# Laying the score masks of the second half of the heads with ScalarE instead of VectorE

## The chip, the core and the metric

The kernel runs on one core of a Trainium2 chip. The metric is the device time of one execution in microseconds (us), lower is better. One execution of the kernel before was also taken with the hardware profiler; all readings of single instructions come from it. PE is TensorE, PEld its weight loads, DVE is VectorE, ACT is ScalarE, POOL is GpSimd, SP is SyncE, which issues most DMAs.

## What is computed

Two layers of the same kind, one after the other: a recurrent attention with a small memory, and a dense block, each with a residual. Between segments the attention is sequential: the memory that segment s leaves is part of the input of segment s+1.

```python
def A(x, mem0, Wq, Wk, Wv, Wo):          # S=2048, Dm=512, H=32 heads of Dh=128, M=8, seg=32
    mask = (idx[:, None] < M) | (idx[:, None] >= idx[None, :])     # 40 x 40
    mem = mem0
    for s in range(64):
        h = concat([mem, x[32*s : 32*s+32]])                       # 40 rows
        q, k, v = h @ Wq, h @ Wk, h @ Wv                           # per head
        scores = where(mask, q @ k.T * Dh**-0.5, -1e9)
        o = (softmax(scores) @ v) @ Wo
        mem = o[:M];  outs.append(o[M:])
x = x + A(layernorm(x));  x = x + relu(layernorm(x) @ w1) @ w2     # w1: 512 x 1376
x = x + A(layernorm(x));  x = x + relu(layernorm(x) @ w1) @ w2     # the same weights again
```

## The kernel before

**Steps.** The kernel makes 68 steps k = 0 to 67. In step k the first layer works on segment k and the second layer on segment k-4 (DELTA, line 18), so that both recurrences run side by side. Steps 0 to 3 have the first layer alone, 64 to 67 the second alone; the 60 steps 4 to 63 have both, and are called two-layer steps here. A matrix product then serves both layers at once: its moving operand has 80 columns (two times 40) instead of 40.

**Halves and batches.** The 32 heads are taken in two halves of 16 (`hf` = 0 and 1). For each half `qk` (line 546) makes the queries and keys in three batches of 6, 6 and 4 heads (line 544). A batch n (`qk_batch`, line 524) is a group of Wq products into one PSUM bank, copied to SBUF as QT by ACT (line 538), and a group of Wk products into another bank, copied as KT by DVE (line 540). The banks come from the pool `ps_c`, which has three (line 60); six groups of a half go through these three banks, so each group from the fourth on must wait until an earlier one has been copied out. In the second half of a step the instructions as built, with their waits, give this pairing: the Wk products of the second batch wait for ACT's copy of the first batch, the Wq products of the third batch wait for ACT's copy of the second batch, and the Wk products of the third batch wait for DVE's copy of the first batch. The changed kernel has the same three waits.

**Masks and scores.** Each layer has one score bank (`sp_tiles`, made in lines 208 to 213), 128 partitions by 320 columns of float32, held for the whole kernel. Before the scores are made, a mask (0 or -30000) is copied into the bank from the bf16 tile `maskb2` (`masks`, line 556), and the score products (`scores`, line 560, products in line 566) are then added onto it. `softmax` (line 577) reads the bank twice on DVE: the row maximum (line 582) and the subtraction of it into the SBUF tile `es` (line 586). ACT takes the exponential (line 588), DVE the row sums (line 593), reciprocals (line 594), and POOL or DVE the product with them (line 598). After the subtraction the score bank is free for the next mask.

**Where the masks stand.** The masks of the first half are laid at the end of the step before, in `normalize_step` (line 270, and line 804 for step 0). Those of the second half are laid inside `qk(1, ...)`, lines 552 and 553: the first layer's after batch 1 of the three, the second layer's after batch 2.

**Order.** PE, DVE, SP and POOL keep the order in which the program is written (lines 950 and 951). ACT is not among these: the framework orders ACT's instructions itself, with those made under `high_priority` (`PRIO`, line 19) ahead of others. In step k the first half is made by `qk(0)`, `scores`, `softmax` (lines 856 to 870); then `qk(1)` (line 880), some dense or output products (lines 881 to 887), and `scores` and `softmax` of the second half (lines 889 and 890). So the exponentials of the first half and the copies of the second half's queries stand close together in ACT's queue.

Of the kernel before, what the change touches and what calls it, by code (L numbers as in the profile page):

```python
# [22 lines left out]
def kernel(  # L23
# [14 lines left out]
    nc = tc.nc  # L38
# [138 lines left out]
    maskb2 = maskb[:].unsqueeze(1).to_broadcast([128, 8, L])  # L177
# [30 lines left out]
    sp_banks, sp_tiles = [], []  # L208
# [59 lines left out]
    def normalize_step(k):  # L268
        mom = stat_tail(stats_all) if norm_parts(k) else None
        masks(*layers(k))  # L270
        def rows():
            for eng, R, lo, hi in norm_parts(k):
                normalize(eng, XN, R, mom, lo, hi)


        if len(layers(k)) == 1:
            norm_rows[k] = rows
        else:
            rows()
# [244 lines left out]
    def qk_batch(n, h0, nh, a_lo, a_hi, between=None):  # L524
        ncol = (a_hi - a_lo) * L
        res = []
        for W_sb, nm in ((Wq_sb, "QT"), (Wk_sb, "KT")):
            qp = ps_c.tile([128, HB, 2 * L], F32, tag="c")
            for hi in range(nh):
                h = h0 + hi  # L530
                for c4 in range(NC4):
                    nc.tensor.matmul(qp[:, hi, 0:ncol], lhsT=W_sb[:, c4, h * Dh:(h + 1) * Dh],  # L532
                                     rhs=HT[:, c4, a_lo:a_hi, :], start=(c4 == 0), stop=(c4 == NC4 - 1))
            dst = wk.tile([128, nh, 2 * L], BF, tag=f"{nm}{n}", bufs=1, name=nm)
            if nm == "QT":
                if between:
                    between()
                nc.scalar.copy(out=dst[:, 0:nh, a_lo * L:a_hi * L], in_=qp[:, 0:nh, 0:ncol])  # L538
            else:
                nc.vector.tensor_copy(out=dst[:, 0:nh, a_lo * L:a_hi * L], in_=qp[:, 0:nh, 0:ncol])  # L540
            res.append(dst)
        return res
# [3 lines left out]
    def qk(hf, act, between=None, behind=None):  # L546
        res = []
        for n, (o, nh) in enumerate(BATCHES):
            res.append((o, nh) + tuple(qk_batch(n, 16 * hf + o, nh, act[0], act[-1] + 1, None if n else between)))
            if n == 0 and behind:  # L550
                behind()
            if hf and n > 0:
                masks(*act[n - 1:n])
        return res

    def masks(*act):
        for a in act:
            nc.vector.tensor_copy(out=sp_tiles[a], in_=maskb2)  # L558

    def scores(qks, act):  # L560
        for a in act:
# [237 lines left out]
    def first_step():  # L799


        slots = iter([w1_flat[:, 512 * i:512 * i + 512] for i in range(NC4 * Dff // 512)] +
                     [w2_flat[:, 512 * i:512 * i + 512] for i in range(8)])
        masks(0)
        with tc.high_priority(offset=PRIO):
            qks = qk(0, [0])
            scores(qks, [0])
            softmax(0, [0], True)
# [9 lines left out]
            values0(3, 2, stage=next(slots))  # L818
            load_x(1)
            qks = qk(1, [0], between=lambda: values0(5, 0, stage=next(slots)))  # L820
            scores(qks, [0])
            softmax(1, [0], True)
# [18 lines left out]
    def step(k):  # L841
# [9 lines left out]
        with tc.high_priority(offset=PRIO):  # L851
            behind = norm_rows.pop(k, None)
            if k == 1:
                def behind():
                    normalize(nc.vector, xbs[n_x], xbs[n_x], moments_x(n_x), 0, 128)
            qks = qk(0, act, behind=behind)
            load_values(k, act)
            if k == 1:
                memory_values(k)
                inputs_T(n_x, True)  # L860
# [169 lines left out]
```

## Time and profile before

| | us |
|---|---|
| median of 3 runs | 1603.49 |
| the runs | 1601.55 to 1604.02 |
| the profiled execution, its own time | 1601.33 |
| its span, first to last instruction | 1599.6 |
| PE busy in it | 1568.4 |
| DVE busy | 1262.8 |
| ACT busy | 737.9 |
| POOL busy | 346.7 |

The mean granted clock of TensorE was 0.998 of full speed. In the listings, a row of the timeline gives start, length, engine, line, operation, output and inputs, the count of instructions merged into it, and in brackets the idle time before it with what ended that. The length of an instruction reaches into the start of the next one on its engine where two run back to back, so the difference of two starts is what one costs an engine that has more to do.

### The profile page before, as it was taken

The page shows a single profiled execution, that of the slowest core. Times are in us where ns is not written, and L with a number is a line of the kernel's source. Part 1 is how long each engine was busy: PE and PEld are TensorE (multiplying, and loading weights), DVE is VectorE, ACT ScalarE, POOL GpSimd, SP SyncE. Part 2 cuts the span into 40 slices and gives each one's busy share as a digit, 9 for nine tenths or more (in the row PEclk, how much of TensorE's full clock was granted, in tenths as well). Part 3 has the DMA queues.
Part 4 walks back from the last instruction along what each step waited for, and adds up shares of the span by engine and source line. Part 5 has one row for each costly group of instructions (what it writes and reads, how often), then busy time and mean ns, then how long its engine had stood idle before and what let it go on. Part 6 is the DMA issues. An engine that isn't in the chain of part 4 may idle for free.

```text
span 1599.6 us, 94752 instructions
## 1 busy us (share of the span) xinstructions
PE 1568.4 (98%) x42718; PEld 1323.1 (83%) x42718; DVE 1262.8 (79%) x3112; ACT 737.9 (46%) x1800; POOL 346.7 (22%) x666
## 2 busy tenths in 40 slices
PE   5999999999999999999999999999999999999998
PEld 3677888888888888888888888888888898888876
DVE  4578888888888888888888888878888888787865
ACT  3434444444544444454444445445444544545442
POOL 2012222222222222222222222222222222222210
PEclk9999999999999999999999999999999999999999
DMA  9733343343344434434333433343343333334231
GB/s 367 238 78 77 72 94 85 68 91 86 88 66 91 88 65 93 86 80 75 91 86 64 96 86 81 77 90 89 64 101 81 79 77 80 87 67 100 70 68 38
DMA packets 222532, 146.38 MB, mean 92 GB/s; under 512 B 123976, under 2 KB 216496, under 8 KB 222128
## 3 DMA queue, kind: packets, MB, share of 16 engines
q1 hardware_dynamic: 218976, 136.09, 37.7%
q8 instruction: 335, 5.49, 1.5%
q0 software_dynamic: 3072, 4.20, 1.2%
q14 instruction: 69, 0.57, 0.1%
q10 hardware_dynamic: 80, 0.03, 0.0%
HBM read 65.41 MB, written 45.35 MB: 69 GB/s over the span
## 4 chain that ended last, share of the span: by engine, by line
PE 95%; DMA 2%; DVE 1%; SPq 1%; issue 1%; ACT 1%; POOLq 0%; ACTq 0%; DVEq 0%
PE qp L532 37%; PE wox L365 10%; PE wo L574 8%; PE vm L717 7%; PE v L346 7%; PE hp L468 6%; PE sp L491 5%; PE pv L634 4%; PE sp L566 4%; PE vp L306 3%; DMA Wv_sb<-in_A_Wv_dram 2%; PE tp L608 1%; PE xp L439 1%; PE wox L388 1%; SPq L134 0%
## 5 line engine op out<-in xcount | busy, mean ns | idle before, releaser
L538 ACT CAST QT<-qp 128x480 bf16<-128x480 f32 (+3 forms) x408 | 201.1, 493 | 392.9 <-PE qp L532 390.6
L532 PE MATMUL qp<-HT,Wk_sb 128*128 128x80 bf16 (+1 forms) x8704 | 369.3, 199 | 2.3 <-DVE KT L540 1.3
L532 PE MATMUL qp<-HT,Wq_sb 128*128 128x80 bf16 (+1 forms) x8704 | 369.6, 200 | 1.5 <-POOL HT L706 1.2
L532 PEld LDWEIGHTS <-Wq_sb 128*128 128x128 bf16 x8704 | 326.1, 99 | 32.9 <-issue 25.6
L532 PEld LDWEIGHTS <-Wk_sb 128*128 128x128 bf16 x8704 | 328.5, 100 | 3.8 <-issue 2.7
L540 DVE CAST KT<-qp 128x480 bf16<-128x480 f32 (+3 forms) x408 | 225.0, 565 | 100.8 <-PE qp L532 98.6
L598 POOL TENSOR_TENSOR P_sb<-es,sm 128x320 bf16<-128x320 f32 x185 | 130.6, 719 | 753.0 <-ACT es L588 510.4
L365 PE MATMUL wox<-Wo_sb,OTx 128*64 128x256 bf16 x2880 | 173.6, 273 | 0.0
L582 DVE TENSOR_REDUCE mx<-sp 128x8 f32<-128x320 f32 x256 | 114.8, 487 | 72.6 <-PE sp L566 71.7
L593 DVE TENSOR_REDUCE sm<-es 128x8 f32<-128x320 f32 x256 | 118.9, 464 | 45.4 <-ACT es L588 35.4
L365 PEld LDWEIGHTS <-OTx 128*64 128x64 bf16 x2880 | 150.2, 110 | 2.9
L588 ACT ACTIVATE es<-es 128x320 f32<-128x320 f32 x256 | 110.5, 468 | 57.9 <-DVE es L586 57.2
L717 PE MATMUL vm<-Wv_sb,HTm 128*32 128x512 bf16 x2176 | 136.2, 380 | 0.6 <-DVE HT L786 0.6
L346 PE MATMUL v<-Wv_sb,xnT 128*32 128x512 bf16 x2048 | 129.2, 378 | 0.2 <-issue 0.2
L574 PE MATMUL wo<-Wo_sb,OTm 128*32 128x512 bf16 x2144 | 128.7, 380 | 0.0
L558 DVE CAST sp<-maskb 128x320 f32<-128x320 bf16 x256 | 118.3, 484 | 0.0
L586 DVE TENSOR_TENSOR es<-sp,mx 128x320 f32<-128x320 f32 x256 | 113.7, 483 | 1.5
L717 PEld LDWEIGHTS <-HTm 128*32 128x32 bf16 x2176 | 90.3, 96 | 27.7 <-issue 12.6
L491 PE MATMUL sp<-w_sb,hT 128*64 128x256 bf16 (+4 forms) x1474 | 105.6, 276 | 0.6 <-ACT hT L474 0.5
L468 PE MATMUL hp<-xnT,w_sb 128*128 128x64 bf16 (+3 forms) x2948 | 103.4, 194 | 0.6 <-ACT xnT L986 0.3
L721 ACT CAST VmS<-vm 128x512 bf16<-128x512 f32 x134 | 78.4, 585 | 53.8 <-PE vm L717 53.8
L468 PEld LDWEIGHTS <-w_sb 128*128 128x128 bf16 (+1 forms) x2948 | 96.3, 101 | 1.8 <-issue 1.2
(113 smaller groups left out, 2025.4 us busy)
## 6 DMA issues: line engine op xcount, KB each, us to landing
Vs<-vd SPq DMA_DIRECT2D x96, 256.0 KB
vd<-vst SPq DMA_DIRECT2D x181, 128.0 KB
vmd<-VmS SPq DMA_DIRECT2D x134, 128.0 KB
Vs<-vmd SPq DMA_DIRECT2D x254, 32.0 KB
Vs<-vmd SPq DMA_DIRECT2D x60, 128.0 KB
Wq_sb<-in_A_Wq_dram SPq DMA_DIRECT2D x2, 2048.0 KB
Wk_sb<-in_A_Wk_dram SPq DMA_DIRECT2D x2, 2048.0 KB
Wv_sb<-in_A_Wv_dram SPq DMA_DIRECT2D x2, 2048.0 KB
```

The lines of the kernel that those rows point to most:

```text
L346: nc.tensor.matmul(vp[32 * j:32 * j + 32, :], lhsT=tokens[:, c4, :], rhs=Wv_sb[:, c4, n * 512:(n + 1) * 512], start=(c4 == 0), stop=(c4 == ...
L365: nc.tensor.matmul(out[64 * j:64 * j + nr, 0:256], lhsT=lhsT, rhs=rhs[:, 256 * j:256 * j + 256], start=start, stop=stop, tile_position=(0, ...
L468: nc.tensor.matmul(hp[0:fs, fc - f0, 0:n], lhsT=w1_sb[:, c4, fc * 128:fc * 128 + fs], rhs=cols(c4), start=(c4 == 0), stop=(c4 == NC4 - 1))
L491: nc.tensor.matmul(sp_banks[bank][64 * j:64 * j + n, 0:w], lhsT=hT_tiles[d][0:fs, fc, 0:n], rhs=w2_flat[0:fs, fc * Dm + 256 * j:fc * Dm + ...
L532: nc.tensor.matmul(qp[:, hi, 0:ncol], lhsT=W_sb[:, c4, h * Dh:(h + 1) * Dh], rhs=HT[:, c4, a_lo:a_hi, :], start=(c4 == 0), stop=(c4 == NC4 ...
L538: nc.scalar.copy(out=dst[:, 0:nh, a_lo * L:a_hi * L], in_=qp[:, 0:nh, 0:ncol])
L540: nc.vector.tensor_copy(out=dst[:, 0:nh, a_lo * L:a_hi * L], in_=qp[:, 0:nh, 0:ncol])
L558: nc.vector.tensor_copy(out=sp_tiles[a], in_=maskb2)
L574: nc.tensor.matmul(wo[32 * j:32 * j + 32, :], lhsT=OTm[:, h, n, 2 * M * c:2 * M * c + 4 * M], rhs=Wo_sb[:, h, :], start=(h < 4), stop=(h > ...
L593: nc.vector.tensor_reduce(out=sm[:], in_=es[:], axis=AX.X, op=ALU.add)
L598: eng.tensor_tensor(out=P, in0=es[:], in1=sm[:].unsqueeze(2).to_broadcast([128, 8, L]), op=ALU.mult)
L717: nc.tensor.matmul(vp[32 * j:32 * j + 32, :], lhsT=HTm[:, c4, :], rhs=Wv_sb[:, c4, n * 512:(n + 1) * 512], start=(c4 == 0), stop=(c4 == NC ...
```

## The change

The second half's masks get ScalarE's copy in place of VectorE's. The first layer's mask (the first of `act`) is laid after batch 0 instead of batch 1, the second layer's after batch 1 instead of batch 2. The masks of the first half stay as they are.

```diff
             res.append((o, nh) + tuple(qk_batch(n, 16 * hf + o, nh, act[0], act[-1] + 1, None if n else between)))
             if n == 0 and behind:
                 behind()
-            if hf and n > 0:
-                masks(*act[n - 1:n])
+            if hf:
+                masks(*act[n:n + 1], copy=nc.scalar.copy)
         return res
 
-    def masks(*act):
+    def masks(*act, copy=nc.vector.tensor_copy):
         for a in act:
-            nc.vector.tensor_copy(out=sp_tiles[a], in_=maskb2)
+            copy(out=sp_tiles[a], in_=maskb2)
```

In the program as built, 128 copies leave DVE's queue and 128 come into ACT's. Nothing else changes its place on any engine. In each of the 60 two-layer steps ACT's queue then reads: QT copy of batch 0, two exponentials, the two masks, QT copy of batch 1, QT copy of batch 2. In the one-layer steps it has one exponential and one mask, in steps 1, 2, 3 and 64 to 67 ahead of the QT copy of batch 1.

## Prediction

> **What bounds the kernel now.** I read the page first, then windows of 100 us for the share of each engine, then the waits of PE, and last the timelines of PE and ACT in one two-layer step.
>
> ```profile
> span 1599.6 us, 94752 instructions
> PE 1568.4 (98%) x42718; PEld 1323.1 (83%) x42718; DVE 1262.8 (79%) x3112; ACT 737.9 (46%) x1800; POOL 346.7 (22%) x666
> ...
> PE 95%; DMA 2%; DVE 1%; SPq 1%; issue 1%; ACT 1%; POOLq 0%; ACTq 0%; DVEq 0%
> ```
>
> PE is busy for 98% of the span, and 95% of the chain that ended last is PE. The windows say where the other 2% lies: of 400 to 500 us PE is busy 99.99 us, of 1000 to 1100 us 99.97, of 1300 to 1400 us 100.00. The idle 31 us are mostly in the start, before the weights are there. So in the 60 two-layer steps time is won only where a product takes less time or waits less, and every wait that is put before PE is paid in full. DVE, from which the change takes work, bounds nothing there:
>
> ```profile
> DVE KT L540 <- PE qp L532: 98.6, 135, 5.3
> DVE mx L582 <- PE sp L566: 71.7, 136, 1.5
> ```
>
> It waits 99 us for PE's queries and keys, and 72 us for the scores. In the other direction all waits of PE after the start are small: for DVE's KT 1.5 us in 6 times, for DVE's part of the probabilities 2.1 us in 3.
>
> Now the place of the change. In the step that starts at 787 us the second half's queries and keys run from 792.91 us (ACT first, then PE, then DVE; start, length, engine, line):
>
> ```profile
> 794.03 0.56 ACT L538 CAST QT<-qp 128x480 bf16<-128x480 f32 x1 [2.12 <-PE qp L532]
> 794.49 0.83 ACT L588 ACTIVATE es<-es 128x320 f32<-128x320 f32 x2
> 795.75 0.56 ACT L538 CAST QT<-qp 128x480 bf16<-128x480 f32 x1 [0.43 <-PE qp L532]
> 797.19 0.42 ACT L538 CAST QT<-qp 128x320 bf16<-128x320 f32 x1 [0.88 <-PE qp L532]
> ```
>
> ```profile
> 792.91 1.03 PE L532 MATMUL qp<-HT,Wq_sb 128*128 128x80 bf16 x24
> 793.78 1.03 PE L532 MATMUL qp<-HT,Wk_sb 128*128 128x80 bf16 x24
> 794.64 1.03 PE L532 MATMUL qp<-HT,Wq_sb 128*128 128x80 bf16 x24
> 795.50 1.03 PE L532 MATMUL qp<-HT,Wk_sb 128*128 128x80 bf16 x24
> 796.37 0.73 PE L532 MATMUL qp<-HT,Wq_sb 128*128 128x80 bf16 x16
> 796.93 0.74 PE L532 MATMUL qp<-HT,Wk_sb 128*128 128x80 bf16 x16
> ```
>
> ```profile
> 796.23 1.17 DVE L540 CAST KT<-qp 128x480 bf16<-128x480 f32 x2
> 797.31 0.48 DVE L558 CAST sp<-maskb 128x320 f32<-128x320 bf16 x1
> 797.71 0.49 DVE L540 CAST KT<-qp 128x320 bf16<-128x320 f32 x1
> 798.12 0.48 DVE L558 CAST sp<-maskb 128x320 f32<-128x320 bf16 x1
> ```
>
> Look at the second QT copy. It ends at 795.75 + 0.56 = 796.31, and PE's third Wq group, which takes over the bank that this copy empties, starts at 796.37. PE would have come there at 795.50 + 0.86 = 796.36 anyhow (a group of 24 takes 0.86 from start to start). So there is no slack: what ACT is late with this copy, PE is late with this group. The one-layer steps show that PE really waits there: in step 3 the copy ends at 97.49 us, the third Wq group starts at 97.54, and the group before it took 0.66 where its neighbours took 0.60.
>
> **The change, part by part.**
>
> *DVE loses 128 mask copies* of 0.48 us. I cost this at nothing. After the first mask the third KT copy waits for PE anyway (the last of its 16 products starts near 797.47 and the copy at 797.71), and after the second mask DVE idles until the maxima at 798.88. Should the cover be gone, that is, should PE come earlier, the most to be had is what PE now waits for DVE, under 4 us in all.
>
> *The masks come earlier.* Each needs the subtraction of its layer to be over. ACT's exponentials, ahead of the masks in its queue, wait for the same subtractions, so no new wait is added to ACT, and nobody else uses the bank before the scores at 798.47. The scores no longer wait for DVE's masks; they follow the third KT copy and other products anyway.
>
> *ACT gets two masks between the second exponential and the second QT copy.* Queued behind them: that QT copy, and behind it PE's third Wq group. The free time there: of the two exponentials the second is 0.47 long (mean of its row 468 ns), so it starts at 794.49 + 0.83 - 0.47 = 794.85, and one costs ACT 0.37 from start to start (median of 105 such pairs 372 ns). ACT is free for another from 794.49 + 0.74 = 795.23, and the QT copy starts at 795.75: 0.52 us.
>
> What a mask costs ACT is nowhere in the trace, since ACT never writes PSUM here. Bounds from rows of 320 columns: the slope of ACT's copies is 0.83 ns per column (512 columns 585 ns, 320 columns 425 ns), so 320 columns alone are 0.27, with nothing for starting; the bank-to-SBUF copies, which start the next one early (480 columns 0.46 from start to start, less 160 x 0.83 ns), give 0.32; the exponential, the only one of them that reads SBUF, 0.37; and its whole length, if a write to PSUM let nothing overlap, 0.47. A mask reads SBUF, so it is nearest to the exponential: I take 0.37.
>
> Two masks: 0.74, less the 0.52 that are free, makes the QT copy 0.22 late, and PE with it. PE's third Wk group, which waits for the first KT copy (over near 796.84), comes at 796.93 + 0.22 and finds its bank free. All later in the step hangs on PE: scores, softmax, probabilities, memory, the next step. With PE busy for 99.97 of 100 us no idle stretch takes the 0.22 up. The third QT copy had 0.88 idle before it and stays with PE.
>
> How many times: read step by step, 54 of the two-layer steps have these times within 0.02 us. In three (23, 27, 30) the exponentials come late in the batch and the same sum gives 0.27; in three (45, 48, 52) PE already loses something there, and 0.13, 0 and 0.11 are added. 54 x 0.22 + 3 x 0.27 + 0.24 = 13 us. In the one-layer steps there is one mask: step 3's exponential starts at 96.28, so ACT is free at 96.28 + 0.74 = 97.02, before its QT copy at 97.13: nothing. Step 0 lies under the loading of the weights: nothing.
>
> The sum: 1601.33 + 13 = 1614.3 for the profiled execution (span 1612.6). The median of the runs lies 2.2 above that execution; from it the sum is 1616.5. I give 1615.5, between the two.
>
> At this place the Trainium skill speaks for a smaller cost. "ScalarE: Activation LUTs", section "Step-by-step: what each stage is for", says that ScalarE is closer to PSUM than to SBUF, and that PSUM is the quicker destination. "Perfetto Trace Analysis", section "Optimizing Scalar/DVE Operations", has some 51 ns of overhead for ScalarE on PSUM and 93 on SBUF; the trace agrees for the side that is read (0.32 and 0.37 less 0.27), and shows nothing of the side that is written. By the PSUM figure the sum would be an estimated 7 us.
>
> **The rivals.**
>
> *Forecast, the masks cost PE about 0.22 a step:* 1610 to 1622 us. Chance 0.63.
>
> *A cheap write:* at 0.32 each the QT copy is 0.64 - 0.52 = 0.12 late, 7 us in all: 1608.3 to 1610.5 us. For it: the bank-to-SBUF rows, which also touch a bank. Against it: those read the bank and write SBUF, the reverse of a mask. Chance 0.17.
>
> *No stall:* at 0.26 or less both masks fit into the 0.52. That is below the slope alone. In the middle, up to 0.29, the loss is under 3 us: 1601 to 1605 us. Chance 0.10.
>
> *A dear write:* at 0.47 with no overlap the copy starts at 795.32 + 0.94 = 796.26, 0.51 late, 30 us: 1632 to 1634 us. For it: DVE's own masks into the bank are as long as 0.48. Against it: everything on ACT overlaps its successor by 0.1. Chance 0.06.
>
> *Faster:* DVE, 79% busy, gets 62 us lighter, and PE's waits for DVE shrink. This decides if a mask costs ACT under 0.26 and if the waits of PE for KT and probabilities come from masks in front of them. The price is at most the 1.5 + 2.1 us that PE waits: 1598 to 1600 us. Against it: in the step shown no DVE instruction between the masks and PE's next need is late. The skill, same section of "Perfetto Trace Analysis", advises moving work to ScalarE when DVE is saturated. By that rule, this case; but DVE waits for PE here, so the trace does not meet its condition. Chance 0.04.
>
> **How the numbers follow.** The likeliest is 1615.5. The range takes in the cheap write and part of the small loss below, and above a mask at 0.42 (0.32 late, 19 us, 1620 to 1623): 1605 to 1624. Left out are most of the no-stall case, the faster one and the dear one, together about 0.18. A measurement of this kernel can tell about 0.2%, 3.2 us, from no change. Faster 0.04; same 0.10; slower 0.63 + 0.17 + 0.06 = 0.86.
>
> **What the new profile would show.** ACT: two mask rows of 0.42 to 0.47 between the exponentials and the second QT copy, and no idle time before that copy. PE: in the second half, 1.08 instead of 0.86 from the start of the second Wk group to the third Wq group, the other groups as before, and a new wait of PE line 532 for ACT QT. DVE: about 62 us less busy, and longer waits for PE. Wrong would be: the QT copy still ahead of PE's need (masks are cheap), or a loss at another place, for instance at the scores.

## The result, and the profile after

The changed kernel took 1621.1 us, median of five runs (1617.95 to 1621.29), where the kernel before took 1604.02 in five runs (1601.55 to 1605.51): ratio 1.010, 95% interval 1.0088 to 1.0112. A second set of runs (e8 below) gave 1615.96 against 1601.09, ratio 1.0093 (1.0079 to 1.0106). So it is slower by 0.9 to 1.0%, 15 to 17 us, where the sum of the prediction had 13. The 1621.1 lies in the range of 1605 to 1624, 5.6 above the likeliest time. The first profiled execution took 1621.22 us:

```profile
span 1619.5 us, 94753 instructions
...
PE 1580.8 (98%) x42718; PEld 1325.3 (82%) x42718; DVE 1217.9 (75%) x2984; ACT 777.4 (48%) x1928; POOL 347.6 (21%) x666
```

DVE got 45 us lighter and the kernel 20 us longer in this execution: the engine that was relieved was not the one that set the time. DVE's two longest waits grew by 63 us, about its 45 us less of work and the 20 us more of time together:

```profile
DVE KT L540 <- PE qp L532: 134.1, 203, 5.3
DVE mx L582 <- PE sp L566: 99.1, 135, 1.5
```

They were 98.6 and 71.7 before. PE's busy time grew by 12.4 us (1568.4 before) for the same 42718 products; why is said below. Now the step that corresponds to the one of the prediction. ACT first, then PE, then DVE (start, length, engine, line):

```profile
804.95 0.56 ACT L538 CAST QT<-qp 128x480 bf16<-128x480 f32 x1 [2.12 <-PE qp L532]
805.40 0.83 ACT L588 ACTIVATE es<-es 128x320 f32<-128x320 f32 x2
806.13 0.78 ACT L558 CAST sp<-maskb 128x320 f32<-128x320 bf16 x2
806.84 0.56 ACT L538 CAST QT<-qp 128x480 bf16<-128x480 f32 x1
808.28 0.43 ACT L538 CAST QT<-qp 128x320 bf16<-128x320 f32 x1 [0.88 <-PE qp L532]
```

```profile
805.55 1.03 PE L532 MATMUL qp<-HT,Wq_sb 128*128 128x80 bf16 x24
806.41 1.03 PE L532 MATMUL qp<-HT,Wk_sb 128*128 128x80 bf16 x24
807.45 0.73 PE L532 MATMUL qp<-HT,Wq_sb 128*128 128x80 bf16 x16
808.02 0.74 PE L532 MATMUL qp<-HT,Wk_sb 128*128 128x80 bf16 x16
...
809.56 0.56 PE L566 MATMUL sp<-KT,QT 128*40 128x40 bf16 x32
```

```profile
810.03 0.89 DVE L582 TENSOR_REDUCE mx<-sp 128x8 f32<-128x320 f32 x2 [0.74 <-PE sp L566]
```

The second QT copy has no idle time in brackets any more: it starts as soon as the masks let it, at 806.84, and ends at 807.40. PE's third Wq group starts at 807.45, 1.04 us after the second Wk group, where it was 0.86 or 0.87. That is the stall that was forecast. There is a second loss, which was not. From the first score product (809.56) to the first maximum (810.03) there are 0.47 us; before it was 798.47 to 798.88, 0.41:

```profile
798.47 0.56 PE L566 MATMUL sp<-KT,QT 128*40 128x40 bf16 x32
798.88 0.89 DVE L582 TENSOR_REDUCE mx<-sp 128x8 f32<-128x320 f32 x2 [0.28 <-PE sp L566]
```

The page hardly shows the first loss. Its list of waits has PE waiting for ACT's QT for 2.4 us in 6 times (1.7 in 3 in the second profile), not for 60 x 0.176. The row of a product is 0.20 us long although the next one starts 0.036 later, so the last Wk product, which starts 220 ns ahead of the third Wq group where it was 43 before, reaches to within 18 ns of it. The stall stands under PE's busy time. It is found by the distance of starts, not by idle time.

In nanoseconds, as medians over the 60 two-layer steps, each point counted from the step's own start:

| point of the step | later than before, ns, first profile | second profile |
|---|---|---|
| second Wk group of the second half | 0 | 0 |
| third Wq group | 176 | 175 |
| first score product | 176 | 175 |
| first maximum | 246 | 244 |
| first transpose of the probabilities | 226 | 226 |
| first product with the values | 245 | 244 |
| next step | 245 | 243 |

So a two-layer step costs 176 ns at the QT copy and 69 ns between the scores and the maxima, and 60 x 0.245 = 14.7 us in all. In the one-layer steps the maxima come 69 to 70 ns later too. What the first profile has above that in the 60 steps (together 17.0) lies in single steps; there it is a different one in each execution. The rest of the span is 2.9 us longer, and I did not take it apart. The second profile's 60 steps come to 14.9.

### The profile page after: what moved, and what is told of

It is laid out like the page before. It is cut to its first block, busy times and chain, and to the rows that moved or that the text cites. A ratio compares the mean times of both kernels' runs of the same rounds, so it can differ in the third digit from the quotient of the medians.

```text
span 1619.5 us, 94753 instructions
## 1 busy us (share of the span) xinstructions
PE 1580.8 (98%) x42718; PEld 1325.3 (82%) x42718; DVE 1217.9 (75%) x2984; ACT 777.4 (48%) x1928; POOL 347.6 (21%) x666
## 5 line engine op out<-in xcount | busy, mean ns | idle before, releaser
L532 PEld LDWEIGHTS <-Wq_sb 128*128 128x128 bf16 x8704 | 329.6, 99 | 44.8 <-issue 31.3
L222 POOL TENSOR_TENSOR rstd<-rstd,mhalf_t 128x1 f32<-128x1 f32 x83 | 46.3, 558 | 224.2 <-DVE rstd L221 224.2
```

## The experiments

All times stand against runs of the kernel before made beside them on the same chip; in parentheses is the 95% interval of the ratio. The kernel before took 1601 to 1602 us beside e1 to e8, where the expected times count from about 1603; so e1, e2, e4 and e8 lie up to 1.0 us below the ranges that they were given, while their differences from the kernel before (10.6, 3.7, 3.7 and 14.9) are those expected.

**The two costs, taken away one by one.** For e1 the changed kernel gets one small copy after the second KT copy:

```diff
             if hf:
                 masks(*act[n:n + 1], copy=nc.scalar.copy)
+            if hf and n == 1:
+                nc.vector.tensor_copy(out=probe[:], in_=sp_banks[act[-1]][:, 0:1])
```

> The changed kernel, and VectorE copies one column of the last mask bank into a scratch tile after the second KT copy of the half (128x1, 68 times). VectorE has then seen ScalarE's masks, and the maxima of the second half wait for PE alone instead of for PE and then ScalarE. Theory (two costs in each two-layer step of the changed kernel: 0.176 us because the QT copy is late behind the masks, and 0.069 us because the maxima start later after the scores, by a second wait in front of them): the gap from the first score product to the first maximum goes back from 0.486 to 0.418 us, the 0.176 at the third Wq group stays, so 60 x 0.176 = 10.6 us over the kernel before, 1613 to 1616 us. Rival (all of it is the work that ScalarE has more): as the changed kernel, 1618 to 1621, or a little more for the added copies.

Measured: 1612.61 against 1601.99, ratio 1.0062 (1.0048 to 1.0077), 7.7 to 12.3 us. PE, then DVE, in one step:

```profile
822.36 1.03 PE L533 MATMUL qp<-HT,Wk_sb 128*128 128x80 bf16 x24
823.40 0.73 PE L533 MATMUL qp<-HT,Wq_sb 128*128 128x80 bf16 x16
...
825.99 0.57 PE L569 MATMUL sp<-KT,QT 128*40 128x40 bf16 x32
```

```profile
824.17 0.15 DVE L556 COPY probe<-sp 128x1 f32<-128x1 f32 x1
...
826.40 0.49 DVE L585 TENSOR_REDUCE mx<-sp 128x8 f32<-128x320 f32 x1 [1.17 <-PE sp L569]
```

The stall at the third Wq group is still there (1.04 us between the groups), the gap to the maximum is back at 0.41 (median 0.417). A copy of 0.15 us more on DVE has made the kernel faster than the changed one. This work on DVE costs nothing; a wait in the wrong place does.

For e2 the masks go behind the second QT copy. It does not help to write them later in the program: with the masks written after batches 1 and 2, as before, but on ScalarE, the built queues of all engines are those of the changed kernel, because the framework orders ACT itself and puts forward what is ready. So their order is fixed by an edge (`issue_after`), which orders them in ACT's queue without a wait:

```diff
-            if hf:
-                masks(*act[n:n + 1], copy=nc.scalar.copy)
+            if hf and n == 1:
+                with tc.issue_after(qt_copy[-1].ins):
+                    masks(*act, copy=nc.scalar.copy)
```

> Both masks on ScalarE, but queued behind the QT copy of the second batch (their order fixed by an edge without a semaphore), where ScalarE sits idle 0.88 us before the third QT copy. Theory: the third Wq group comes as in the kernel before, the second wait of the maxima stays, 60 x 0.069 = 4 us over the kernel before, 1606 to 1610 us. Rival (the work on ScalarE): as the changed kernel, 1617 to 1621.

Measured: 1605.72, ratio 1.0019 (1.0008 to 1.0030), 1.3 to 4.8 us. The rival is out. ACT, then PE and DVE, in one step:

```profile
843.18 0.56 ACT L538 CAST QT<-qp 128x480 bf16<-128x480 f32 x1 [0.48 <-PE qp L532]
843.63 0.79 ACT L560 CAST sp<-maskb 128x320 f32<-128x320 bf16 x2
844.61 0.42 ACT L538 CAST QT<-qp 128x320 bf16<-128x320 f32 x1 [0.19 <-PE qp L532]
```

```profile
842.92 1.02 PE L532 MATMUL qp<-HT,Wk_sb 128*128 128x80 bf16 x24
843.79 0.73 PE L532 MATMUL qp<-HT,Wq_sb 128*128 128x80 bf16 x16
...
846.37 0.68 PE L568 MATMUL sp<-KT,QT 128*40 128x40 bf16 x32
```

```profile
846.86 0.89 DVE L584 TENSOR_REDUCE mx<-sp 128x8 f32<-128x320 f32 x2 [1.24 <-PE sp L568]
```

The same two masks on the same engine lie in its idle time, the groups are 0.87 apart again, and the 0.49 to the maximum stays.

> Both together: masks on ScalarE behind the second QT copy, and VectorE reads one column of the bank after its third KT copy, so that the maxima wait for PE alone. Theory: neither cost, 1602 to 1606 us, as the kernel before. Not faster, because VectorE was not what PE waited for. Rival (the work on ScalarE): 1617 to 1621. Rival (a lighter VectorE is worth something once the new waits are gone): under 1601.

Measured: 1603.67, ratio 1.0008 (0.9999 to 1.0017). With both costs gone the third Wq group and the maxima are where they were before (medians 0 and 1 ns apart), and the step as long (4 ns shorter). Moving 62 us of masks from VectorE to ScalarE is then worth nothing, which was the forecast's reading of DVE.

**How much of ScalarE's work.** For e4 the first layer's mask alone goes to ScalarE:

> The first layer's mask on ScalarE after batch 0, the second layer's on VectorE after batch 2. Theory: one mask of 0.35 us fits into the 0.52 us that ScalarE has before the QT copy, so nothing at the third Wq group; the first maximum keeps its second wait, 60 x 0.069 = 4 us, 1606 to 1610. Rival (the work on ScalarE, by its amount): half of the loss, 1611 to 1613, with 0.09 us at the third Wq group.

Measured: 1605.68, ratio 1.0022 (1.0012 to 1.0032), 1.9 to 5.1 us; half of the loss would be 7 to 8. The median step is 66 ns longer, all of it at the maxima, and the third Wq group has lost 1 ns:

```profile
822.77 0.83 ACT L590 ACTIVATE es<-es 128x320 f32<-128x320 f32 x2
823.50 0.43 ACT L560 CAST sp<-maskb 128x320 f32<-128x320 bf16 x1
824.04 0.56 ACT L538 CAST QT<-qp 128x480 bf16<-128x480 f32 x1
```

One mask fits: 823.50 + 0.355 = 823.86, and the QT copy, which PE's products release, comes at 824.04. For e6 each mask is laid twice:

> The changed kernel with each of ScalarE's masks laid twice in a row, so four copies stand ahead of the QT copy. Theory: a mask costs ScalarE 0.35 us, so the QT copy comes at exp + 0.37 + 4 x 0.35 after the second exponential, 0.87 us late instead of 0.175, and PE with it: 60 x 0.70 = 42 us over the changed kernel, 1659 to 1665. Rival (an ordinary share of ScalarE's work, ScalarE is busy for half of the time only): under 1635.

Measured: one run, 1642.47 against 1601.09, so 41 us, less than I expected and more than the rival. The reason is in the queue. The framework put three of the four masks ahead of the QT copy and the fourth behind it:

```profile
838.25 0.83 ACT L589 ACTIVATE es<-es 128x320 f32<-128x320 f32 x2
838.98 1.14 ACT L559 CAST sp<-maskb 128x320 f32<-128x320 bf16 x3
840.05 0.56 ACT L538 CAST QT<-qp 128x480 bf16<-128x480 f32 x1
840.50 0.44 ACT L559 CAST sp<-maskb 128x320 f32<-128x320 bf16 x1
```

A mask takes 0.355 from start to start. The second exponential starts 1.953 us after PE's first group of the half and the QT copy came at 2.845 before. With three masks it is 1.953 + 0.360 + 3 x 0.357 = 3.384, 0.54 late; measured at the third Wq group 0.533, and with the maxima 0.60 a step: 36 us of the 41. The line of one, two and three masks (1, 176, 533 ns) has its corner where the forecast put it, at the end of ACT's free 0.52.

**Place or engine.** For e5 the masks are laid early as in the change, but by VectorE:

> The place of the changed kernel with the engine of the kernel before: masks on VectorE after batches 0 and 1. Theory (the cost comes with ScalarE: its queue ahead of the QT copy, and a wait for a second engine ahead of the maxima): no wait of PE changes, the maxima wait as in the kernel before, 1600 to 1605 us, same. Rival (the earlier place is what costs): 1617 to 1621.

Measured: 1602.53 against 1601.09, ratio 1.0007 (0.9998 to 1.0016), and no point of the median step moves by more than 3 ns. The place costs nothing.

**What makes the maxima late.** In the programs as built, before and after, this maximum has two waits. One is held by a separate instruction in front of it, the other by the maximum itself. Before: VectorE's own mask in front, PE on the maximum. After: PE in front, ScalarE on the maximum, although ScalarE has long been done. (In e1 and e3 it waits for PE alone.) The traces have the separate instruction too. After, in the median, it starts 422 ns after the first score product, which is when the maximum itself started before (417), and the maximum starts 64 to 65 ns behind it. So either the order matters, or the second engine. To separate the two, the masks stay as they were before, and another engine writes one column of the tile that the maxima overwrite: ScalarE in e9, POOL in e10 (both come behind PE in the order of waits), a DMA in e11 (it comes ahead).

```diff
+                    nc.scalar.copy(out=mx_second[a][:, 0:1], in_=zero8[:, 0:1])        # e9
+                    nc.gpsimd.tensor_copy(out=mx_second[a][:, 0:1], in_=zero8[:, 0:1]) # e10
+                    nc.sync.dma_start(out=mx_second[a][:, 0:1], in_=zero8[:, 0:1])     # e11
```

> The kernel before with its masks on VectorE; only, in the two-layer steps, ScalarE copies one column of zeros into each tile that the second half's maxima then overwrite (two copies of 128x1, behind the second QT copy where ScalarE is idle). The maxima now wait for VectorE and PE in front and for ScalarE last. Theory (a late wait that stands in front of the instruction, and not on it, costs 0.069 us): gap from first score product to first maximum 0.486 us, 60 x 0.069 = 4 us, 1604 to 1608. Rival (the 0.069 comes from the mask's own write into the bank, or from VectorE's idle time where its mask stood): gap 0.418, no change.

> The same with POOL in place of ScalarE (two copies of 128x1 at the head of each two-layer step): the maxima wait for VectorE and PE in front and for POOL last. Theory: gap 0.486 us and about 4 us more, as with ScalarE. Rival (it is something of ScalarE's): gap 0.418, no change.

> The same with a DMA in place of ScalarE (two of 512 bytes on SP's queue at the head of each two-layer step): the maxima wait for the DMA and VectorE in front and for PE last, that is for more than in the other two, but with the late wait on the instruction itself. Theory (it is the place of the late wait): gap 0.418 us, no change, 1600 to 1604, if the two DMAs delay nothing else. Rival (it is the number of engines that are waited for): gap 0.486 or more, 4 us or more.

Measured against 1602.36: e9 1606.62, ratio 1.0023 (1.0014 to 1.0032); e10 1605.96, ratio 1.0019 (1.0009 to 1.0028); e11 1611.94, ratio 1.0059 (1.0038 to 1.0079). The gap to the first maximum is 473 ns in e9 and e10 and 418 in e11; the median step is 55 ns longer in e9 and e10 and 1 ns in e11. First e9, then e11, at the same step:

```profile
824.06 0.57 PE L574 MATMUL sp<-KT,QT 128*40 128x40 bf16 x32
824.53 0.89 DVE L590 TENSOR_REDUCE mx_second<-sp 128x8 f32<-128x320 f32 x2 [0.82 <-issue]
```

```profile
830.34 0.57 PE L569 MATMUL sp<-KT,QT 128*40 128x40 bf16 x32
830.76 0.49 DVE L585 TENSOR_REDUCE mx_second<-sp 128x8 f32<-128x320 f32 x1 [0.77 <-PE sp L569]
```

All three have one wait more than the kernel before. In e9 and e10 the separate instruction holds VectorE's wait and PE's; it ends 429 ns after the first score product, and the maximum follows 43 ns behind its end, as it does in the changed kernel. In e11 it holds the DMA's and VectorE's, and PE's is on the maximum. Only those are late in which PE, which ends last, is waited for in front. So it is the order. The masks have no part in it, and ScalarE none of its own. No run here has PE's wait on the maximum beside one for ScalarE or POOL, so that a wait for these two costs something by itself is not excluded by a run. The trace of the kernel before speaks against it: 308 of ScalarE's QT copies have PE's wait in a separate instruction and a wait for ScalarE's own work on the copy, and they too start 39 to 45 ns behind the end of that instruction. The gap was 473 ns in e9 and e10, not the 486 that I expected.

My time for e11 was wrong: its two DMAs a step did delay something else. Its loss lies in some 15 single steps of 0.3 to 1.7 us; in seven of them the page of waits has PE at the dense products waiting for the DMA transpose of XN, 4.8 us in all. The rest I did not trace.

**The same rule at another place: a miss.** The first transpose of the probabilities waits for two engines, too. In e7 a product of one element, four products earlier, takes one of the waits away:

```diff
+            dense_y(k - 2, 0, f_mid - 2)
+            nc.tensor.matmul(sp_banks[0][0:1, 504:505], lhsT=P1_sb[:, 0:1], rhs=ident[:, 0:1], ...)
+            dense_y(k - 2, f_mid - 2, f_mid)
```

> The kernel before, with the rule of the second wait turned to use at another place. The first transpose of the second half's probabilities (weight load of P1) waits for VectorE and POOL, with the later one, VectorE, in a wait of its own ahead of the load. A product of one element in the 60 two-layer steps, put four products earlier, reads POOL's part of P1, so that the load waits for VectorE alone. Theory: the load comes about 0.07 us sooner after VectorE's product, up to 60 x 0.07 = 4 us less than the kernel before, less some 0.05 us for the added product where PE doesn't wait: 1597 to 1602, ratio 0.996 to 1.000. Rival (a separate wait costs only VectorE): no gain, ratio 1.000 to 1.002.

Measured: 1609.1 against 1601.09, ratio 1.0055 (1.0042 to 1.0069).

```profile
804.40 0.96 PE L491 MATMUL sp<-w_sb,hT 128*64 128x320 bf16 x14
805.29 0.16 PE L902 MATMUL sp<-ident,P_sb 128*1 128x1 bf16 x1
805.39 0.41 PE L491 MATMUL sp<-w_sb,hT 128*64 128x256 bf16 x4
805.63 0.45 PE L608 MATMUL tp<-ident,P_sb 128*64 128x80 bf16 x16
```

The transposes follow the last dense product by 106 ns, and did so in the kernel before, by 107 in the median: in most steps they were waiting for PE's own products, not for the probabilities. (In about every fourth step they did wait for the probabilities; there the added product puts PE behind as well.) So the rule is not tested here, and the added product makes the median last dense product 215 ns late. It is written for PE as one piece, between products written for one half of it each (`tile_position`). The Trainium skill, "TensorEngine Tiling (Array Packing)", section "Key Properties", says that a change of the tiling mode drains TensorE; 0.2 us for one element agrees with that, though no run here separates it from the product itself.

> The changed kernel once more, beside the others on the same chip: 1617 to 1621 us by both. Theory: third Wq group 0.175 us late in each two-layer step, maxima 0.069 us later after the scores, 60 x 0.245 = 14.7 us, ratio about 1.009; what is above that differs from execution to execution and lies in single steps.

Measured: 1615.96, ratio 1.0093 (1.0079 to 1.0106), and the second column of the table above.

## Why the prediction was right, and where it was not

*What bounds the kernel* held. PE is busy throughout, DVE's relief is worth nothing (e3), and a stall of PE in a step is paid in full: the 176 ns of the third Wq group are still there at the scores, and in e1 at the next step (170). But a PE that is busy for 99.97 of 100 us does not show that it has no stalls: in the changed kernel it is busy for 99.57 to 99.87 in the same windows, with a stall of 0.176 us in each step.

*The masks on ACT, the QT copy, PE's third Wq group*: the mechanism was right, and e1, e2, e4 and e6 bear it out. Its size was somewhat too large. I had 0.37 a mask and 0.22 a step; measured were 0.355 and 0.176, the latter because the first mask also follows the exponential by 0.360 instead of 0.37. 60 x 0.176 = 10.6 us, not 13. The choice of the exponential as the nearest row was good to 5%. That fits a cost that goes by the side that is read; no run here varies the side that is written alone. The bound from the bank-to-SBUF copies (0.32) was too low. The Trainium skill's 51 ns for ScalarE on PSUM, in "Perfetto Trace Analysis", section "Optimizing Scalar/DVE Operations", would have had an estimated 0.318; the measured 0.355 less 0.267 for the columns leaves 88 ns, which is near its 93 for SBUF, the side that a mask reads.

*"The masks come earlier", with no new wait,* is the step that failed. I looked for new waits on ACT and on PE and found none, and put this part of the change at nothing. The new wait was on the reader of the bank: DVE's maxima wait for whoever laid the mask, and that was DVE itself before, so the wait cost nothing. With another engine as writer the wait for PE moved into a separate instruction ahead of the maximum, and each maximum came 69 ns later after its scores. The maxima stand at the head of a chain (maximum, subtraction, exponential, sum, product, transpose) that ends on PE. Of the 69 ns, 50 reach the first transpose and all the first product with the values. ("A loss at another place, for instance at the scores" was one of the prediction's own signs of being wrong; 0.069 of the 0.245 us of a step is such a loss.) That is 60 x 0.069 = 4.1 us, and with the 10.6 it makes 14.7. The Trainium skill, "Perfetto Trace Analysis", section "Identifying Dependency Chains", says that an instruction that waits for several engines may get separate instructions with the further waits ahead of it. The programs here agree; it does not say that their order costs time, which e9 to e11 show.

*The sum* came near partly by luck, since the two errors are of opposite sign: 2.4 us too much at ACT, 4.1 us left out at DVE.

*Cheap write, no stall, dear write:* a mask at 0.355 rules them out. *Faster:* e3, with VectorE relieved and both costs gone, is not faster than the kernel before, by a ratio of 0.9999 at the least.

*What the profile would show* held for ACT (mask rows of 0.43, no idle time before the QT copy) and in the main for PE (1.04 between the groups instead of 1.08). The new wait of PE for ACT's QT is there by the starts of the products, but hardly in the list of waits, as said above. DVE is 45 us less busy, not 62: the masks' lengths lay partly over those of their neighbours, and the page counts such time once.

Open stays what stops single steps. In step 5 of the first profile PE pauses inside a group of products, with nothing shown that it waits for:

```profile
141.87 0.85 PE L532 MATMUL qp<-HT,Wk_sb 128*128 128x80 bf16 x19
142.90 0.34 PE L532 MATMUL qp<-HT,Wk_sb 128*128 128x80 bf16 x5 [0.18 <-issue]
```

Such steps are there before and after, each time others (23 and 30 before; 5, 26, 27 and 31 after), and I made no experiment on them.

## What to carry to other kernels

An engine that is idle for half of the time can have no time at all where it is needed: before moving work to it, find the copy behind which the saturated engine stands, and measure the idle time just ahead of that copy (here 0.52 us, with room for one mask of 0.355, not two). When work on a tile goes to another engine, list the waits of its readers as well as those of its writer, and look which wait stands on the instruction itself. The wait that ends last should stand there; a cheap read on the same engine, placed earlier, takes the other one away.

## What the runs showed of the hardware

ScalarE writing a 128x320 float32 score bank from a bf16 SBUF tile takes 425 ns by its row, and 355 ns from start to start when it has more to do; VectorE's copies of the same masks take 484. On VectorE's maxima, a wait that ends last costs 55 to 69 ns more when it is held by a separate instruction in front than when the maximum holds it itself (gap 473 and 486 ns instead of 417 or 418), whether the other wait is for ScalarE or for POOL. The number of waits made no difference: 418 with three, the late one last, and 417 with one or two. A stall of PE of 176 ns in each of 60 steps stood almost wholly under its busy time (12.4 us more for the same products), since a row of these products is 202 ns long and the next one starts after 36.
